# VectorE's order written out for the whole ramp, one pair of maxima moved into the ramp, and weight loads due in slots 5 to 12 issued in slot 13

## The chip, the cores and the metric

The kernel runs on one core of one Trainium2 chip. The metric is the device time of one execution in microseconds (us). The kernel before takes 1043.43 us (median of 3 runs, 1042.8 to 1046.78).

## The reference

Two branches share one layer norm, and both are added to the input:

```python
xn = _layernorm(x, axis=-1)                       # x: 2048 tokens x 640
return x + _A_ref(xn, A_wqkv, A_wo) + _B_ref(xn, B_w_gate, B_w_up, B_w_down)
```

Branch A is attention with 32 heads of 20 columns; each query sees the 256 keys up to and including its own:

```python
scores = jnp.einsum("bhqd,bhkd->bhqk", q, k) * (Dh ** -0.5)
mask = (idx[:, None] - idx[None, :] >= 0) & (idx[:, None] - idx[None, :] < W)   # W = 256
p = _softmax(jnp.where(mask[None, None], scores, -1e9), axis=-1)
```

Branch B is a gated feed-forward part, `h = gelu(g) * u`, of width 1728. All tensors are float32.

## The kernel before

**Stages.** The 2048 tokens are four chunks of 512 (c = 0 to 3). First comes the *ramp* (`first_chunk`, L345, the loop behind it, L460, and twelve steps of filler at the head of `attention()`, L832): layer norm, transposes of the normed tiles, first projections. Then `attention()` (L823) works through 32 *units* u (8 groups of four heads times 4 chunks), each cut into 14 *slots* i; T = 14 u + i counts slots. Dense projections ("filler") are pulled in between so that TensorE (PE) never lacks work. After that come the feed-forward part and the output sums, which the change does not touch.

**Dense products.** An operand is split into a high and a low fp32r part, and `dense_steps` (L104) issues three blocks of five matmuls, weight by input: high by high, low by high, high by low (so `xl` is read in the last block). `proj_qk` (L240) makes one 128-row slice of q (t below 5) or k (t from 5) for a chunk in a PSUM bank `ps_d` (pool `psd`, two banks). `proj_v` (L315) makes `ps_v` for one tile of 128 tokens.

**What follows a projection.** `save_qk` (L248) cuts q or k into three bf16 parts: ScalarE (ACT) writes the first into `pt` (L277), VectorE (DVE) subtracts it into `r` (L273), ACT writes the second (L255), GpSimd (POOL) the third (L259), and SyncE (SP) stores `pt` to DRAM (`qd` or `kd`, L268). `r` has one buffer, so the next L273 waits until POOL has read the last one; `pt` has two, so an L277 waits for the store of the tile before last. `load_stack` (L478) reads q and k back from DRAM into `qs` (three buffers) and `ks` (four) three units ahead, in slots 9 (`ks`) and 12 (`qs`).

**Layer norm in the ramp.** Per tile of 128 tokens `xi`, DVE computes statistics (L149 to L151), per chunk the scale (L156 to L165), per tile the normed values (L169). PE transposes them into `ps_t` (L185), ACT writes the high part `xh` (L193), DVE the low part `xl` (L194). In `first_chunk` (L345) every engine's order is written out by hand; after it a scheduler sets the order of all engines in the ramp, mixing statistics of chunks 2 and 3 with other work of DVE.

**Maxima.** `max_pair` (L493) makes two PSUM banks of masked scores `ps_m` (L512, pool `psm`, four banks, shared with transposes), and DVE reduces each to its row maxima (L522). Eight pairs make a unit. Pairs are pulled ahead of the unit in which they serve: by `pull_max` in the ramp's last part (L832: 12 steps of filler, two pairs in each even step) and in slots 0, 5 and 9, twice in slot 0, and once in T = 3. In a slot, `exp_piece` (L563) then issues scores `ps_e` (L577) for ACT's exponentials (L579).

**Weight loads.** When chunk 0 of a filler set is done, `load_qk` (L232) or `load_gu` (L640) at once issues two loads `wr` of 320 KB for the next set on SP, whatever the slot. `split_later` (L651) has ACT read them (L656) once chunk 1, then chunk 2 of the set is done, some 14 slots later each. SP issues all these DMAs in the order of the program, on one queue.

Of the kernel before, what the change touches and what calls it, by code (L numbers as in the profile page):

```python
# [20 lines left out]
NC = S // C  # L21
# [46 lines left out]
def block_kernel(ctx, tc, x, wqk, wv, wgu, wdo, wdl, out):  # L68
# [99 lines left out]
    def ln_apply(xi, mv, rs):  # L168
        nc.vector.tensor_scalar(xi, xi, mv[:, 0:1], rs, op0=OP.subtract, op1=OP.mult)  # L169

    def ln_scale(xs, lp, mv=None, begun=0):
        n = len(xs)
        mv = mv or lp.tile([128, n, 2], F32, name="mv4", tag="mv4", bufs=2)
        for i in range(begun, n):
            ln_stats(xs[i], mv[:, i, :], lp)
        rs = ln_rstd(*ln_sqrt(mv, n, lp), n, lp)
        for i, xi in enumerate(xs):
            ln_apply(xi, mv[:, i, :], rs[:, i:i + 1])

    def turn(k, xs, where):  # L180
        n = len(xs)
        pool, tag = {"x": (psx, "ex"), "m": (psm, "mx"), "o": (psm, "mx")}[where]
        ps = pool.tile([128, n * 128], F32, name="ps_t", tag=tag)
        for i in range(n):
            nc.tensor.transpose(ps[:, i * 128:(i + 1) * 128], xs[i][:, k * 128:(k + 1) * 128], ident)  # L185
        return ps

    def ln_turn(t0, xs, where="xmxmx"):
        n = len(xs)
        cs = slice(t0 * 128, (t0 + n) * 128)  # L190
        for k in range(KT):
            ps = turn(k, xs, where[k])
            nc.scalar.activation(xh[:, k, cs], ps, AF.Copy)  # L193
            nc.vector.tensor_tensor(out=xl[:, k, cs], in0=ps, in1=xh[:, k, cs].bitcast(F32), op=OP.subtract)  # L194

    acts = {}
    done = set()
# [27 lines left out]
    def behind(fn, *a):  # L225
# [3 lines left out]
        else:  # L229
            fn(*a)  # L230

    def load_qk(t):  # L232
        raw = wrp.tile([128, KT, 128], F32, name="wr", tag="wr")
        nc.sync.dma_start(raw, wqk[t])
        return raw

    def split_qk(raw):
        return split(wp, raw, [128, KT, 128], "wq", nc.gpsimd)
# [106 lines left out]
    def first_chunk(xs, wr0, wr5, prep, v0, lp):  # L345
        halves = slice(0, 256), slice(256, 512)

        def low(k, ps, cs):
            nc.vector.tensor_tensor(out=xl[:, k, cs], in0=ps, in1=xh[:, k, cs].bitcast(F32), op=OP.subtract)

        def high(k, ps, cs):
            nc.scalar.activation(xh[:, k, cs], ps, AF.Copy)

        def part(ps, w, r, cs, first=False, last=False, ks=range(KT)):
            for k in ks:
                nc.tensor.matmul(ps[:, cs], w[:, k, :], r[:, k, cs], start=first and k == 0,  # L356
                                 stop=last and k == KT - 1, skip_group_check=True)

        def high_qk(raw):
            wh = wp.tile([128, KT, 128], F32R, name="wqh", tag="wqh")  # L360
            nc.scalar.activation(wh, raw, AF.Copy)
            return wh

        def low_qk(raw, wh):
            wl = wp.tile([128, KT, 128], F32R, name="wql", tag="wql")
            nc.gpsimd.tensor_tensor(out=wl, in0=raw, in1=wh.bitcast(F32), op=OP.subtract)
            return wh, wl

        def hold(xi):
            nc.gpsimd.tensor_copy(one[:, 0:1], xi[:, 0:1])  # L370

        with tc.manual_schedule(engines=MANUAL | {mybir.EngineType.Pool}):
            mv = [lp.tile([128, 2, 2], F32, name="mv", tag="mv", bufs=2) for _ in range(2)]
            ln_stats(xs[0], mv[0][:, 0, :], lp)
            ln_stats(xs[1], mv[0][:, 1, :], lp)
            rs = ln_rstd(*ln_sqrt(mv[0], 2, lp), 2, lp)
            ln_apply(xs[0], mv[0][:, 0, :], rs[:, 0:1])
            ln_apply(xs[1], mv[0][:, 1, :], rs[:, 1:2])
            wh0 = high_qk(wr0)
            hold(xs[1])  # L380
            w0 = low_qk(wr0, wh0)
# [36 lines left out]
            part(dn[1], w5[1], xh, halves[1])  # L418
            part(dn[1], wh5, xl, halves[1], last=True)
            mv = lp.tile([128, 4, 2], F32, name="mv4", tag="mv4", bufs=2)  # L420
            for j in range(4):
                ln_stats(xs[4 + j], mv[:, j, :], lp)
            rs = ln_rstd(*ln_sqrt(mv, 4, lp), 4, lp)
            for i in range(2):
                for _ in proj_v(v0, i, (psm, "mx")):
                    pass
            for j in range(4):
                ln_apply(xs[4 + j], mv[:, j, :], rs[:, j:j + 1])
            save_qk(0, 0, dn[0])
            mv = lp.tile([128, 4, 2], F32, name="mv4", tag="mv4", bufs=2)  # L430
            for j in range(2):
                ln_stats(xs[8 + j], mv[:, j, :], lp)
        save_qk(5, 0, dn[1])
        return w0, w5, v0, mv

    v0 = []
    with tc.tile_pool(name="lp", bufs=1, side="right") as lp:
# [15 lines left out]
        w0, w5, v0, mv = first_chunk(xs, wr0, wr5, prep, v0, lp)  # L453
        ones = lp.tile([4, 2 * C], BF, name="ones")
        nc.gpsimd.memset(ones, 0.0)
        nc.gpsimd.memset(ones[0:2], 1.0)
        for i in range(NK):
            for j in (0, 2):
                nc.sync.dma_start(ks[i][SR:64, j:j + 2].rearrange("p j t -> p (j t)"), ones)
        for c in range(1, NC):  # L460
            if c > 1:
                ln_scale(xs[4 * c:4 * c + 4], lp, *((mv, 2) if c == 2 else ()))
            ln_turn(4 * c, xs[4 * c:4 * c + 4], "xmxmx" if c == NC - 1 else "xmxmm")
            if 1 < c < NC - 1:
                xs += [ln_load(t, lp) for t in range(4 * c + 4, 4 * c + 8)]
            if c == 1:
                for i in range(NQ):
                    for j in (0, 2):
                        nc.sync.dma_start(qs[i][SR + 2:64, j:j + 2].rearrange("p j t -> p (j t)"), ones[2:4])
            if c == 2:  # L470
                raws1 = [load_qk(1), load_qk(6)]
            if c < NC - 1:
                run(*[proj_v(v0, 4 * c - 4 + i, None if i % 2 else (psm, "mx")) for i in range(0 if c > 1 else 2, 4)])
                run(proj_qk(0, w0, c), proj_qk(5, w5, c))
# [165 lines left out]
    def load_gu(f):  # L640
        raws = []
        for i in range(2 if f < NF - 1 else 1):
            raw = wrp.tile([128, KT, 128], F32, name="wr", tag="wr")
            nc.sync.dma_start(raw, wgu[2 * f + i])
            raws.append(raw)
        return raws

    def split_gu(pools, raws):
# [174 lines left out]
    def attention():  # L823
# [8 lines left out]
        for i in range(12):  # L832
# [3 lines left out]
            if i == 0:  # L836
                pull_max(1, now[0])
                pull_fill(RAMP)
                pull_max(1, now[0])
                debt[0] -= RAMP  # L840
            elif i % 2 == 0:
                pull_max(2, now[0])
            flush()
            pull_fill(2 * RAMP)
# [688 lines left out]
```

## Time and profile before

| | |
|---|---|
| Median of 3 runs | 1043.43 us |
| Profiled execution, its own time | 1043.06 us |
| Span in the trace | 1041.3 us |
| Time around the span | 1.76 us |
| PE busy | 1031.8 us (99%) |
| VectorE busy | 740.3 us (71%) |
| ScalarE busy | 527.9 us (51%) |
| GpSimd busy | 384.5 us (37%) |

A timeline row reads: start, duration, engine, line, operation, out<-in, count, and in brackets the idle time of that engine just before it and what ended it. A wait row reads: engine and line that waited, what it waited for, the total, the number of waits, the longest. A windows row gives the stretch, then each engine's busy time, the granted PE clock, the busy share of the DMA engines and GB/s. A PE row's duration reaches past the start of the next row, since matmuls are pipelined; the step from start to start is what a row takes of the engine.

### The profile page before, as it was taken

Reading aid. Unit: us, or ns where it says so; the run is one execution under the profiler, and the core shown is the slowest. Engines: PE = TensorE matmul, PEld = TensorE weight load, DVE = VectorE, ACT = ScalarE, POOL = GpSimd, SP = SyncE. Lnnn points to the kernel's source line nnn. Section 1 sums busy time; section 2 is a strip of 40 time slices with the busy share of each in tenths; the row PEclk is TensorE's granted clock in tenths of the full one; section 3 lists DMA queues with packets and bytes.
Section 4 is the critical chain, followed back from the end, with each engine's and each line's share of the span. In section 5 each row is a group of like instructions: output and inputs, shape, how many; then the busy total and the mean of one; then the engine's idle time right before and its main releaser. Section 6 shows DMA issues by size and latency. Waiting matters only on the chain.

```text
span 1041.3 us, 25568 instructions
## 1 busy us (share of the span) xinstructions
PE 1031.8 (99%) x9396; PEld 834.4 (80%) x9396; DVE 740.3 (71%) x2018; ACT 527.9 (51%) x1120; POOL 384.5 (37%) x623
## 2 busy tenths in 40 slices
PE   9999999999999999999999999999999999999998
PEld 8887666666777666666678888888888999999998
DVE  7855666677656576777736778776556888888887
ACT  4434766767666666666675322223324544333332
POOL 5122778988765787766461111101110000000000
PEclk9999999999999999999999999999999999999999
DMA  6642356564633455343325576673117874433333
GB/s 224 182 144 70 110 157 182 160 181 142 185 98 99 117 150 163 94 145 109 99 76 190 187 248 212 246 256 110 72 58 268 252 244 138 137 128 111 127 122 105
DMA packets 102150, 158.74 MB, mean 152 GB/s; under 512 B 14172, under 2 KB 55260, under 8 KB 102024
## 3 DMA queue, kind: packets, MB, share of 16 engines
q1 hardware_dynamic: 99640, 150.94, 45.7%
q10 hardware_dynamic: 2384, 6.16, 1.9%
q8 instruction: 74, 1.21, 0.5%
q14 instruction: 52, 0.43, 0.1%
HBM read 101.78 MB, written 54.92 MB: 150 GB/s over the span
## 4 chain that ended last, share of the span: by engine, by line
PE 92%; DVE 5%; DMA 1%; issue 1%; ACT 1%; SPq 0%; DVEq 0%; ACTq 0%
PE ps_g L977 24%; PE ps L1249 23%; PE ps_d L108 19%; PE ps_e L577 8%; PE ps_v L108 6%; PE ps_o L620 5%; PE ps_m L512 5%; DVE junk L522 2%; PE ps_g L108 1%; PE ps_d L356 1%; DVE xi L169 0%; DMA qs<-qd 0%; PE ps_t L185 0%; DVE st L150 0%; DVE xl L194 0%
## 5 line engine op out<-in xcount | busy, mean ns | idle before, releaser
L522 DVE CUSTOM_DVE_ANT_0 junk<-ps_m,mask 128x320 bf16<-128x320 f32 (+2 forms) x512 | 242.5, 474 | 132.1 <-PE ps_m L512 73.6
L579 ACT ACTIVATE P<-ps_e 128x512 f32<-128x512 f32 (+2 forms) x384 | 198.7, 572 | 65.3 <-PE ps_e L577 64.6
L1249 PE MATMUL ps<-wb,at 128*128 128x320 f32 x999 | 155.9, 309 | 0.0
L1249 PEld LDWEIGHTS ps<-wb,at 128*128 128x128 f32 x999 | 148.9, 188 | 0.2
L592 POOL TENSOR_SCALAR_AFFINE_SELECT P<-P 128x256 f32<-128x256 f32 (+1 forms) x192 | 94.7, 495 | 72.4 <-ACT P L579 71.6
L577 PE MATMUL ps_e<-qs,ks 124*128 124x128 bf16 (+2 forms) x704 | 118.3, 278 | 0.1
L108 PE MATMUL ps_d<-xl,wqh 128*128 128x512 f32 x310 | 98.5, 421 | 0.0
L108 PE MATMUL ps_d<-xh,wqh 128*128 128x512 f32 x310 | 98.3, 421 | 0.0
L108 PE MATMUL ps_d<-xh,wql 128*128 128x512 f32 x310 | 97.6, 418 | 0.0
L101 POOL TENSOR_TENSOR wql<-wr,wqh 128x640 fp32r<-128x640 f32 x12 | 19.2, 1607 | 195.4 <-PE ps_g L977 150.8
L1249 PE MATMUL ps<-wt,at 128*128 128x320 f32 x552 | 88.9, 309 | 0.0
L577 PEld LDWEIGHTS <-ks 124*128 124x128 bf16 x704 | 49.5, 98 | 49.0 <-issue 34.4
L1249 PEld LDWEIGHTS ps<-wt,at 128*128 128x128 f32 x552 | 82.9, 188 | 0.1
L595 POOL TENSOR_SCALAR_AFFINE_SELECT P<-P 128x512 f32<-128x512 f32 (+1 forms) x144 | 76.8, 542 | 16.3 <-ACT P L579 16.3
L1203 ACT ACTIVATE at<-ss 128x512 fp32r<-128x512 f32 x59 | 37.3, 632 | 83.3 <-DVE ss L1082 83.3
L620 PE MATMUL ps_o<-P,v 64*32 64x320 f32 (+4 forms) x2816 | 74.2, 347 | 0.0
L259 POOL TENSOR_TENSOR pt<-r,pt 128x512 bf16<-128x512 f32 x40 | 46.7, 1167 | 64.4 <-ACT pt L255 64.0
L620 PEld LDWEIGHTS ps_o<-P,v 64*32 64x32 f32 x2816 | 50.8, 106 | 21.5 <-issue 0.9
L512 PE MATMUL ps_m<-ks,qs 60*64 60x320 bf16 (+3 forms) x1472 | 64.0, 260 | 3.2 <-DMA qs<-qd 1.1
L108 PEld LDWEIGHTS ps_d<-xh,wql 128*128 128x128 f32 x310 | 56.0, 189 | 10.2 <-issue 1.3
L1006 ACT ACTIVATE hr<-hr 128x512 f32<-128x512 f32 x20 | 12.6, 632 | 101.6 <-DVE hr L980 101.6
L108 PEld LDWEIGHTS ps_d<-xh,wqh 128*128 128x128 f32 x310 | 56.0, 189 | 9.8 <-issue 1.6
(197 smaller groups left out, 1981.6 us busy)
## 6 DMA issues: line engine op xcount, KB each, us to landing
hd<-he SPq DMA_DIRECT2D x50, 256.0 KB
hr<-hd SPq DMA_DIRECT2D x48, 256.0 KB
wr<-wgu SPq DMA_DIRECT2D x27, 320.0 KB
qs<-qd SPq DMA_DIRECT2D x64, 120.0 KB
ks<-kd SPq DMA_DIRECT2D x64, 120.0 KB
xi<-x SPq DMA_DIRECT2D x16, 320.0 KB
qs<-qd SPq DMA_DIRECT2D x64, 80.0 KB
ks<-kd SPq DMA_DIRECT2D x64, 80.0 KB
```

What stands on the lines that cost most here:

```text
L108: nc.tensor.matmul(ps, a(k), b(k), start=n == 0, stop=n == 3 * nk - 1)
L259: nc.gpsimd.tensor_tensor(out=pt[:, l, :], in0=r, in1=pt[:, 1, :], op=OP.subtract)
L512: nc.tensor.matmul(ps[64 * h:64 * h + 64, col:col + w], q[rows, j, q0:q0 + 64], ks_, start=True, stop=True, tile_position=(64 * r, 64 * h))
L522: nc.vector.tensor_tensor_reduce(out=junk[:, 0:n], in0=ps[:, 320 - n:320], in1=mask[:, 320 - n:320], scale=1.0, scalar=NEG, op0=OP.add, op ...
L577: nc.tensor.matmul(ps[:, col:col + n], k[0:QROWS, j, kc:kc + 128], q[0:QROWS, j, q0:q0 + n], start=True, stop=True)
L579: nc.scalar.activation(pt[:, j, lo:hi], ps[:, lo:hi], AF.Exp, scale=SCALE)
L592: nc.gpsimd.affine_select(out=a, in_=a, pattern=[[0, n], [1, 128]], compare_op=OP.is_ge, fill=0.0, base=0, channel_multiplier=-1)
L595: nc.gpsimd.affine_select(out=a, in_=a, pattern=[[0, n], [-1, 128]], compare_op=OP.is_ge, fill=0.0, base=-1, channel_multiplier=1)
L620: nc.tensor.matmul(os[r][32 * j:32 * j + 32, qa:qb], v[rows, w0_:w0_ + 32], pt[rows, j, col + qa - q0:col + qb - q0], start=r not in begun ...
L977: nc.tensor.matmul(ps, i, j, start=first and n == 0, stop=n == len(work) - 1, skip_group_check=True)
L1203: nc.scalar.activation(hi[:, 3:7], s, AF.Copy)
L1249: nc.tensor.matmul(ps[bank][:, 0:HD], *work[bank][j], start=bank not in begun, stop=final[p, bank] == n and j == len(work[bank]) - 1, skip ...
```

## The change

Four edits. (1) In the ramp after `first_chunk`, DVE's order is now the program's. The program text is rearranged so that statistics of a chunk's first two tiles (`ln_begin`) come in fixed places, the rest of the layer norm of chunk c + 1 (`ln_scale`) right behind chunk c's `xl`, and the second part of k's first slice (`save_qk(5, 0)`) between the third and fourth `xl` of chunk 1. (2) The fifth transpose of chunk 3 goes to a bank of pool `psd` ("d") and not `psx`. (3) Two pairs of maxima are pulled in the ramp's last step (i = 11), and none in T = 3. (4) A load `wr` that falls due in slots 5 to 12 is issued in slot 13 of the same unit.

```diff
-    def ln_scale(xs, lp, mv=None, begun=0):
+    def ln_begin(xs, lp):
+        mv = lp.tile([128, 4, 2], F32, name="mv4", tag="mv4", bufs=2)
+        for i in range(2):
+            ln_stats(xs[i], mv[:, i, :], lp)
+        return mv
+
+    def ln_scale(xs, lp, mv):
         n = len(xs)
-        mv = mv or lp.tile([128, n, 2], F32, name="mv4", tag="mv4", bufs=2)
-        for i in range(begun, n):
+        for i in range(2, n):
             ln_stats(xs[i], mv[:, i, :], lp)
...
+    def load_later(src):
+        raw = wrp.tile([128, KT, 128], F32, name="wr", tag="wr")
+        i = 0 if now[0] is None or now[0] < 0 else now[0] % NS
+        if i > 4:
+            at(now[0] + NS - 1 - i, lambda: nc.sync.dma_start(raw, src))
+        else:
+            nc.sync.dma_start(raw, src)
+        return raw
...
+            mv = ln_begin(xs[8:], lp)
             save_qk(0, 0, dn[0])
...
-        save_qk(5, 0, dn[1])
-        return w0, w5, v0, mv
+        return w0, w5, v0, mv, dn[1]
...
-        for c in range(1, NC):
-            if c > 1:
-                ln_scale(xs[4 * c:4 * c + 4], lp, *((mv, 2) if c == 2 else ()))
-            ln_turn(4 * c, xs[4 * c:4 * c + 4], "xmxmx" if c == NC - 1 else "xmxmm")
...
+        with tc.manual_schedule(engines={mybir.EngineType.DVE}):
+            for c in range(1, NC):
+                ln_turn(4 * c, xs[4 * c:4 * c + 4], "xmxmd" if c == NC - 1 else "xmxmm",
+                        (lambda: save_qk(5, 0, k_first)) if c == 1 else None)
+                if c == NC - 1:
+                    break
+                ln_scale(xs[4 * c + 4:4 * c + 8], lp, mv)
...
+                run(proj_qk(0, w0, c))
+                if c == 1:
+                    mv = ln_begin(xs[12:], lp)
+                run(proj_qk(5, w5, c))
...
-            elif i % 2 == 0:
+            elif i % 2 == 0 or i == 11:
                 pull_max(2, now[0])
...
-                if i in (0, 5, 9) or T == 3:
+                if i in (0, 5, 9):
                     pull_max(2, T)
```

Three places show how the order of the instructions moves. The first is VectorE in the ramp, at the normalization of chunk 2. `mv_556` (before) and `mv_548` (after) hold chunk 2's statistics, `mv_910` those of chunk 3. Before:

```order
L149 BN_STATS st<-xi 128x6
L163 TENSOR_TENSOR ve<-ve,rs 128x4
L150 BN_STATS st<-xi 128x6
L273 TENSOR_TENSOR r<-ps_d,pt 128x512
L164 SCALAR_TENSOR_TENSOR ve<-ve,rs 128x4
L151 BN_AGGR mv_910<-st 128x2
L149 BN_STATS st<-xi 128x6
L165 SCALAR_TENSOR_TENSOR rs<-ve,rs 128x4
L150 BN_STATS st<-xi 128x6
L169 TENSOR_SCALAR xi<-xi,mv_556,rs 128x640 x3
L273 TENSOR_TENSOR r<-ps_d,pt 128x512
L169 TENSOR_SCALAR xi<-xi,mv_556,rs 128x640
```

And after, where `mv_721` holds chunk 3's statistics:

```order
L151 BN_AGGR mv_548<-st 128x2
L156 TENSOR_TENSOR ve<-mv_548,one 128x4
L162 RECIPROCAL rs<-sq 128x4
L163 TENSOR_TENSOR ve<-ve,rs 128x4
L164 SCALAR_TENSOR_TENSOR ve<-ve,rs 128x4
L165 SCALAR_TENSOR_TENSOR rs<-ve,rs 128x4
L169 TENSOR_SCALAR xi<-xi,mv_548,rs 128x640 x4
L287 TENSOR_TENSOR r<-ps_d,pt 128x512
L149 BN_STATS st<-xi 128x6
L150 BN_STATS st<-xi 128x6
L151 BN_AGGR mv_721<-st 128x2
```

The four normalizations of chunk 2 now stand ahead of both subtractions `r` of chunk 1 and of all statistics of chunk 3. The second place is TensorE behind the ramp's last regular pairs (`ps_m<-ks_180,qs_177`, step i = 10). Before, filler runs up to slot 0 of unit 0, whose pairs begin with `ks_179`:

```order
L512 MATMUL ps_m<-ks_180,qs_177 64x320
L108 MATMUL ps_d<-xl_80,wqh 128x512 x4
L108 MATMUL ps_d<-xh_76,wqh 128x512 x5
L108 MATMUL ps_d<-xh_76,wql 128x512 x5
L108 MATMUL ps_d<-xl_80,wqh 128x512 x5
L108 MATMUL ps_v<-wvh,xh_79 128x320 x5
L108 MATMUL ps_v<-wvh,xl_83 128x320 x5
L108 MATMUL ps_v<-wvl,xh_79 128x320 x5
L108 MATMUL ps_v<-wvh,xh_79 128x320 x5
L512 LDWEIGHTS qs_177
L512 MATMUL ps_m<-ks_179,qs_177 64x256
```

After, the same pairs come eight filler matmuls behind those of i = 10:

```order
L527 MATMUL ps_m<-ks_180,qs_177 64x320
L108 MATMUL ps_d<-xl_80,wqh 128x512 x4
L108 MATMUL ps_d<-xh_76,wqh 128x512 x4
L527 LDWEIGHTS qs_177
L527 MATMUL ps_m<-ks_179,qs_177 64x256
```

All later pairs up to T = 3 move up by one place, and T = 3 has none. The third place is SyncE in unit 4, at the first of the four pairs of loads that move. Before:

```order
L487 DMA ks_182<-kd_91 60x1024
L234 DMA wr<-wqk 128x640 x2
L268 DMA qd_84<-pt 64x3x512 x2
L487 DMA qs_177<-qd_87 40x1024
L487 DMA qs_177<-qd_87 20x1024
L487 DMA qs_177<-qd_87 60x1024
```

After:

```order
L502 DMA qs_177<-qd_87 40x1024
L502 DMA qs_177<-qd_87 20x1024
L502 DMA qs_177<-qd_87 60x1024
L243 DMA wr<-wqk 128x640 x2
L282 DMA kd_88<-pt 64x3x512 x2
L775 DMA td_102<-tx 128x256
```

The two loads are now behind the store `qd_84` and all six `qs_177` loads, and directly ahead of the store `kd_88`. The other three pairs of loads that move (units 8, 12 and 21) also go behind the `qs` loads of their unit.

More of the change, by code (lines that the diff above doesn't have):

```diff
@@ L181, in turn @@
         n = len(xs)
-        pool, tag = {"x": (psx, "ex"), "m": (psm, "mx"), "o": (psm, "mx")}[where]
+        pool, tag = {"x": (psx, "ex"), "m": (psm, "mx"), "o": (psm, "mx"), "d": (psd, "dn")}[where]
         ps = pool.tile([128, n * 128], F32, name="ps_t", tag=tag)
@@ L186, in turn, with ln_turn @@
         return ps
-    def ln_turn(t0, xs, where="xmxmx"):
+    def ln_turn(t0, xs, where, mid=None):
         n = len(xs)
@@ L194, in ln_turn @@
             nc.vector.tensor_tensor(out=xl[:, k, cs], in0=ps, in1=xh[:, k, cs].bitcast(F32), op=OP.subtract)
+            if k == 2 and mid:
+                mid()
     acts = {}
@@ L230, in behind @@
             fn(*a)
+    def load_later(src):
[6 more added lines that the diff above has]
+        return raw
     def load_qk(t):
-        raw = wrp.tile([128, KT, 128], F32, name="wr", tag="wr")
-        nc.sync.dma_start(raw, wqk[t])
-        return raw
+        return load_later(wqk[t])
     def split_qk(raw):
@@ L428, in first_chunk @@
                 ln_apply(xs[4 + j], mv[:, j, :], rs[:, j:j + 1])
+            mv = ln_begin(xs[8:], lp)
             save_qk(0, 0, dn[0])
-            mv = lp.tile([128, 4, 2], F32, name="mv4", tag="mv4", bufs=2)
-            for j in range(2):
-                ln_stats(xs[8 + j], mv[:, j, :], lp)
-        save_qk(5, 0, dn[1])
-        return w0, w5, v0, mv
+        return w0, w5, v0, mv, dn[1]
     v0 = []
@@ L452, in block_kernel @@
         xs += [ln_load(t, lp) for t in range(4, 8)]
-        w0, w5, v0, mv = first_chunk(xs, wr0, wr5, prep, v0, lp)
+        w0, w5, v0, mv, k_first = first_chunk(xs, wr0, wr5, prep, v0, lp)
         ones = lp.tile([4, 2 * C], BF, name="ones")
@@ L459, in block_kernel @@
                 nc.sync.dma_start(ks[i][SR:64, j:j + 2].rearrange("p j t -> p (j t)"), ones)
-        for c in range(1, NC):
-            if c > 1:
-                ln_scale(xs[4 * c:4 * c + 4], lp, *((mv, 2) if c == 2 else ()))
-            ln_turn(4 * c, xs[4 * c:4 * c + 4], "xmxmx" if c == NC - 1 else "xmxmm")
[L464 to L472, printed above, removed]
+        with tc.manual_schedule(engines={mybir.EngineType.DVE}):
[6 more added lines that the diff above has]
+                if c == 1:
+                    xs += [ln_load(t, lp) for t in range(12, 16)]
+                    for i in range(NQ):
+                        for j in (0, 2):
+                            nc.sync.dma_start(qs[i][SR + 2:64, j:j + 2].rearrange("p j t -> p (j t)"), ones[2:4])
+                else:
+                    raws1 = [load_qk(1), load_qk(6)]
                 run(*[proj_v(v0, 4 * c - 4 + i, None if i % 2 else (psm, "mx")) for i in range(0 if c > 1 else 2, 4)])
-                run(proj_qk(0, w0, c), proj_qk(5, w5, c))
+                run(proj_qk(0, w0, c))
+                if c == 1:
+                    mv = ln_begin(xs[12:], lp)
+                run(proj_qk(5, w5, c))
     vtiles = dict(enumerate(v0[2]))
@@ L642, in load_gu @@
         for i in range(2 if f < NF - 1 else 1):
-            raw = wrp.tile([128, KT, 128], F32, name="wr", tag="wr")
-            nc.sync.dma_start(raw, wgu[2 * f + i])
-            raws.append(raw)
+            raws.append(load_later(wgu[2 * f + i]))
         return raws
```

## The prediction

> **What bounds the kernel now.** I read the page's first part, then TensorE's waits, then its timeline around each of them, then the engine or queue that ended each.
>
> ```profile
> PE 1031.8 (99%) x9396; PEld 834.4 (80%) x9396; DVE 740.3 (71%) x2018; ACT 527.9 (51%) x1120; POOL 384.5 (37%) x623
> ```
>
> TensorE (PE) is busy 1031.8 of 1041.3 us, and the change removes none of its matmuls. All that can be won is PE's idle time, 1041.3 - 1031.8 = 9.5 us, and the little that hides in rows stretched by a wait. Its waits, without that for the very first operand:
>
> ```profile
> PE ps_t L185 <- DVE xi L169: 1.2, 3, 0.8
> PE ps_m L512 <- DMA qs<-qd: 1.1, 2, 0.6
> PE ps_m L512 <- DVE mx L522: 0.6, 2, 0.4
> PE ps_t L185 <- DVE xl L194: 0.2, 1, 0.2
> PE ps_m L512 <- DVE xl L194: 0.2, 1, 0.2
> ```
>
> They make 1.2 + 1.1 + 0.6 + 0.2 + 0.2 = 3.3 us; the rest of the idle time has no wait named. The reader sees three that weigh: transposes waiting for normed tiles (edit 1 touches it), maxima waiting for `qs` (edit 4) and for earlier maxima (edit 3); edit 2 touches the fourth row.
>
> **Edit 1, VectorE's order.** PE around the transposes of chunk 1 (24.18) and of chunk 2 (38.56 to 41.25):
>
> ```profile
> 24.18 2.34 PE L185 MATMUL ps_t<-ident,xi 128*128 128x128 f32 x20
> 26.28 0.97 PE L108 MATMUL ps_v<-wvh,xh 128*128 128x320 f32 x5
> ...
> 38.56 2.03 PE L185 MATMUL ps_t<-ident,xi 128*128 128x128 f32 x15 [0.82 <-DVE xi L169]
> 40.35 0.54 PE L108 MATMUL ps_v<-wvh,xh 128*128 128x320 f32 x2
> 40.73 0.77 PE L185 MATMUL ps_t<-ident,xi 128*128 128x128 f32 x5
> 41.25 0.69 PE L108 MATMUL ps_v<-wvh,xh 128*128 128x320 f32 x3
> ```
>
> Unhindered, 20 transposes step 26.28 - 24.18 = 2.10 us. In chunk 2 they step (40.35 - 38.56) + (41.25 - 40.73) = 2.31, after 0.82 of idle time. Excess: 0.82 + 0.21 = 1.03 us. What VectorE (DVE) did before:
>
> ```profile
> 18.98 0.44 DVE L149 BATCH_NORM_STATS2 st<-xi 128x6 f32<-128x320 f32 x1
> ...
> 19.84 0.21 DVE L151 BATCH_NORM_AGGREGATE mv<-st 128x2 f32<-128x12 f32 x1
> ...
> 21.29 2.18 DVE L169 TENSOR_SCALAR xi<-xi,mv,rs 128x640 f32<-128x640 f32 x4
> 26.01 0.69 DVE L273 TENSOR_TENSOR r<-ps_d,pt 128x512 f32<-128x512 f32 x1 [2.54 <-issue]
> ...
> 29.57 2.43 DVE L194 TENSOR_TENSOR xl<-ps_t,xh 128x512 fp32r<-128x512 f32 x4
> ...
> 37.19 2.37 DVE L169 TENSOR_SCALAR xi<-xi,mv,rs 128x640 f32<-128x640 f32 x3
> ```
>
> DVE idles 2.54 us at 23.5. One tile's statistics take 19.84 + 0.21 - 18.98 = 1.07 us, so the two tiles that now come first fit there (2.1 us), and `r` behind them starts where it did, near 26. Chunk 1's two `r` (0.69 each) and five `xl` (0.61 each: 2.43 / 4) take 4.4 us; I add 0.6 because the second `r` must let ACT and POOL finish with the first (one buffer). The `xl` then end near 31 (before: 29.57 + 2.43 = 32.0). Two tiles of statistics 2.1, the scale 1.24 (21.29 - 20.05), four normalizations 2.18: the last is ready near 36.5. PE asks at 38.56 - 0.82 = 37.7. With 1.2 us of slack the **1.03 us** go.
>
> What was pushed back, chunk 1's two `r` of the next projections and chunk 3's first statistics, ends about 36.5 + 2 x 0.69 + 2.1 = 40, and chunk 2's `xl` (five of 0.61) by 43 to 44. PE's reader of those is the last block of the projections that begin here:
>
> ```profile
> 33.05 1.30 PE L108 MATMUL ps_d<-xl,wqh 128*128 128x512 f32 x5
> ...
> 49.84 1.32 PE L108 MATMUL ps_d<-xh,wqh 128*128 128x512 f32 x5
> ```
>
> So they have cover to 50 us; chunk 1's `xl`, ending near 31, to 33.05. The moves cost nothing while that cover stands; past it each us is PE's.
>
> **Edit 2, the bank of the fifth transpose.** It ends one wait and uncovers the next:
>
> ```profile
> 57.62 0.69 DVE L273 TENSOR_TENSOR r<-ps_d,pt 128x512 f32<-128x512 f32 x1 [2.71 <-ACT pt L277]
> 58.23 3.19 DVE L194 TENSOR_TENSOR xl<-ps_t,xh 128x512 fp32r<-128x512 f32 x5
> ...
> 58.97 0.66 PE L185 MATMUL ps_t<-ident,xi 128*128 128x128 f32 x4 [0.20 <-DVE xl L194]
> ...
> 60.88 0.31 PE L512 MATMUL ps_m<-ks,qs 60*64 60x64 bf16 x5 [0.18 <-DVE xl L194]
> ```
>
> At 58.97 the fifth transpose waited for the first `xl` to free its bank. At 60.88 the second pair waited for the fourth `xl` (58.23 + 4 x 0.64 = 60.8). DVE's chain starts with `r`, which waits for ACT behind the end of PE's projection, and that chain is unchanged; PE merely waits longer at the second place. I cost the edit at nothing; bounds 0 and -0.38, the two rows.
>
> **Edit 3, the pairs of T = 3.**
>
> ```profile
> 82.57 0.49 DVE L522 CUSTOM_DVE_ANT_0 junk<-ps_m,mask 128x320 bf16<-128x320 f32 x1
> ...
> 83.22 0.49 DVE L522 CUSTOM_DVE_ANT_0 junk<-ps_m,mask 128x320 bf16<-128x320 f32 x1
> ```
>
> ```profile
> 89.08 0.47 PE L512 MATMUL ps_m<-ks,qs 60*64 60x256 bf16 x16
> 89.48 0.85 PE L108 MATMUL ps_v<-wvh,xl 128*128 128x320 f32 x4
> ...
> 93.50 0.58 PE L512 MATMUL ps_m<-ks,qs 60*64 60x256 bf16 x9
> 94.51 0.33 PE L512 MATMUL ps_m<-ks,qs 60*64 60x128 bf16 x7 [0.43 <-DVE mx L522]
> 94.77 0.39 PE L577 MATMUL ps_e<-qs,ks 124*128 124x256 bf16 x2
> ```
>
> The 16 matmuls of slot 5 step 94.77 - 93.50 = 1.27 us where those of slot 0 step 0.40: one maximum steps 83.22 - 82.57 = 0.65 us, two pairs 2.6, so three pulls in five slots outrun DVE and fill the four banks. Without the pull of T = 3 this is -0.87 us. In step i = 11 the two pairs come eight filler matmuls behind those of i = 10, 2 us by the row at 49.84 (1.32 / 5 each); DVE, which needs 2.6 from the first bank on, may hold the last bank a little longer than PE's own 0.40 allows: 0 to 0.2 lost. Otherwise the pairs cost PE the same there, plus one more change between filler and maxima, 0 to 0.1. I take +0.1 together: **-0.8 us**.
>
> **Edit 4, the loads.** Unit 4, the first of four places, then the `qs` loads of unit 8, where the `wr` loads had gone 5.8 us earlier (213.4) and were through:
>
> ```profile
> 157.91 0.86 SPq L234 DMA_DIRECT2D wr<-wqk  x2
> 158.88 1.32 SPq L268 DMA_DIRECT2D qd<-pt  x2
> 160.30 4.74 SPq L487 DMA_DIRECT2D qs<-qd  x6
> ...
> 219.21 2.14 SPq L487 DMA_DIRECT2D qs<-qd  x6
> ...
> 158.90:161.20 2.30, 2.30 (x85) 1.51 (x86) 1.55 (x7) 0.00 (x0) 2.30 (x4) 1.00 0.98 302
> ...
> 166.32 0.27 PE L512 MATMUL ps_m<-ks,qs 60*64 60x256 bf16 x1 [0.60 <-DMA qs<-qd]
> 167.10 0.47 PE L512 MATMUL ps_m<-ks,qs 60*64 60x256 bf16 x15 [0.51 <-DMA qs<-qd]
> ```
>
> The loads keep the DMA engines 98% busy from 158.9 to 161.2 (640 KB at 302 GB/s are 2.2 us), the six `qs` issues behind them take 4.74 us and not 2.14, and PE then waits 0.60 + 0.51 = **1.11 us** for `qs`. With the loads behind them, `qs` is issued 0.97 us earlier (158.88 - 157.91) and has 2.2 us less traffic ahead: 3 us, more than the wait. The other three places show no wait of PE for `qs`, so nothing there.
>
> The Trainium skill ("DMA: Bandwidth & Descriptors", section "Queues, rings and completion order") says that each DMA engine consumes a ring's descriptors in ring order; the trace agrees, `qs` issues stretching from 2.14 to 4.74 us behind `wr`. By that rule the same 2.2 us move onto the store `kd`, the rival below.
>
> What the loads now delay is ACT, their reader, and the `pt` store behind them:
>
> ```profile
> 227.17 0.59 ACT L277 ACTIVATE pt<-ps_d 128x512 bf16<-128x512 f32 x1
> 227.65 0.73 ACT L656 ACTIVATE wqh<-wr 128x640 fp32r<-128x640 f32 x1
> ```
>
> In unit 8 `wr` will be issued near 219.21 + 2.14 = 221.4, done near 222.3, and take 2.2 us (the rate above) to 4.74 (the stretched issue as a bound): landed by 224.5 to 227, ahead of 227.65. The `kd` store behind it frees the `pt` that ACT writes at 227.17: 2.2 us later than before it can be just late. I take 0; bounds 0 and 2.5 us, in each of units 4 and 8.
>
> **Sum.** -1.03 + 0 - 0.8 - 1.11 = -2.9 us against the profiled 1043.06 us (span 1041.3 and 1.76 around it): **1040.2 us**. The median of the runs, 1043.43, is 0.4 above that execution. The gain is 0.3%, less than the 0.5% (5.2 us) that a measurement of this kernel can tell from no change.
>
> **The rivals.**
> - *The wait for `qs` stays* (the stretched issue has another cause, such as a reader of the buffer): -1.8 us, 1041.2. For it: SP issues `qs` behind other waits as well. Against: the DMA engines are full just then.
> - *Given back at the `pt` store:* the `kd` store, now behind `wr`, lands after ACT wants its `pt` (227.17 in unit 8, the like in unit 4). ACT, its exponentials and PE wait up to 2.5 us in each unit; half of that makes 1040.2 + 2.5 = 1042.7.
> - *Slower: the same store in full.* From 1.5 us of delay in each of the two units the change loses more than its 2.9 us; at 2.5 in each it is 1043.06 - 2.9 + 5.0 = 1045.2. For it: no cover is visible beyond that row of ACT. Against: two units only, and PE holds filler while ACT waits.
> - *A blocked VectorE.* Written out, DVE's order lets a late `r` hold `xl`. If chunk 1's second `r` waits for POOL, its `xl` end later than 31 us, and PE's block at 33.05 needs them: from 2 us of extra wait PE loses each us in full. The nearest row is DVE's 2.71 us for ACT: 0.7 lost there, edit 1's 1.03 not won, 1043.06 - 1.9 + 0.7 = 1041.9. The Trainium skill ("TensorE: Matmul & The Clock Gate", section "What's actually happening") halves PE's clock after an idle window of about 3.4 us; no wait here is longer than 1.2 us and the granted clock is 1.00 in the row at 158.90, so only a longer block would add to it.
> - *Hidden anyway:* each wait returns at the next limit, as in edit 2: 1043.
>
> **Chances.** Forecast (1039.3 to 1040.9) 0.57; `qs` wait stays 0.13; given back 0.10; blocked VectorE 0.05; hidden anyway 0.05; slower 0.05; more than the sum (edit 2's 0.38 and 1.4 of stretched rows like those of edits 1 and 3: 1038.4) 0.05. The range 1038.4 to 1044.0 holds all but the slower case and the noise of a run. Faster by over 0.5% needs 5.2 us where the named waits hold 3.3: the upper part of the last case, 0.04. Slower by over 0.5% needs 8 us of new waits against the gain, the slower case and more of it: 0.04. Within: 0.92.
>
> **What would show it.** Right: no idle time before chunk 2's transposes, their 20 in one row; slot 5 of unit 0 stepping 0.4 us; no wait of PE for `qs`, and PE idle near 7 us. Edit 2 right: the wait at the second pair grows to some 0.4 us. Wrong: ACT's L277 (now L291) waiting for the `kd` store near 170 or 226 us, ACT's read of `wr` waiting, or a gap of PE in 31 to 37 us.

## The result and the profile after

The changed kernel takes 1039.85 us (median of 8 runs, 1039.25 to 1041.25) against 1043.12 us of the kernel before beside it (8 runs): ratio 0.9968, 95% interval 0.9955 to 0.9982. The profiled execution took 1039.31 us, span 1037.6, that is 3.7 us less span than the profiled execution before. The forecast was 1040.2 us and -2.9 us.

The page's first row and TensorE's (PE's) waits after (engine and line that waited, what for, total, times, longest):

```profile
PE 1031.2 (99%) x9396; PEld 834.9 (80%) x9396; DVE 741.0 (71%) x2018; ACT 526.8 (51%) x1120; POOL 383.6 (37%) x623
```

```profile
PE ps_t L190 <- DVE xi L169: 0.2, 1, 0.2
PE ps_m L527 <- DVE xl L199: 0.2, 1, 0.2
```

Without that for the very first operand these are all. PE's idle time fell from 9.5 to 1037.6 - 1031.2 = 6.4 us. The waits for normed tiles (but 0.2 us), for `qs` and for earlier maxima are gone.

**Edit 1.** PE's timeline after, from the last block of chunk 1's projections to chunk 2's first:

```profile
36.29 1.30 PE L108 MATMUL ps_d<-xl,wqh 128*128 128x512 f32 x5
37.43 2.35 PE L190 MATMUL ps_t<-ident,xi 128*128 128x128 f32 x20
39.53 0.98 PE L108 MATMUL ps_v<-wvh,xh 128*128 128x320 f32 x5
...
48.41 1.32 PE L108 MATMUL ps_d<-xh,wqh 128*128 128x512 f32 x5
```

The 20 transposes stand in one row, without idle time, and step 39.53 - 37.43 = 2.10 us. VectorE (DVE) over the same time, from the end of chunk 1's `xl` on:

```profile
28.71 1.28 DVE L199 TENSOR_TENSOR xl<-ps_t,xh 128x512 fp32r<-128x512 f32 x2
...
33.25 2.18 DVE L169 TENSOR_SCALAR xi<-xi,mv,rs 128x640 f32<-128x640 f32 x4
...
38.38 0.69 DVE L287 TENSOR_TENSOR r<-ps_d,pt 128x512 f32<-128x512 f32 x1 [0.32 <-ACT pt L291]
38.98 3.19 DVE L199 TENSOR_TENSOR xl<-ps_t,xh 128x512 fp32r<-128x512 f32 x5
```

Chunk 1's `xl` end at 28.71 + 1.28 = 30.0 us (estimated 31), the last normed tile at 35.4 (36.5), chunk 2's `xl` at 42.2 (43 to 44). PE asks for the normed tiles at 37.43, so they have 2.0 us to spare.

**Edit 2.** Chunk 3's transposes and the first pairs of maxima, after:

```profile
55.24 2.35 PE L190 MATMUL ps_t<-ident,xi 128*128 128x128 f32 x20
...
57.70 1.41 PE L108 MATMUL ps_d<-xh,wqh 128*128 128x512 f32 x4
59.05 0.21 PE L527 MATMUL ps_m<-ks,qs 60*64 60x64 bf16 x1
59.44 0.31 PE L527 MATMUL ps_m<-ks,qs 60*64 60x64 bf16 x5 [0.18 <-DVE xl L199]
```

The wait ahead of the fifth transpose is gone, and the second pair waits 0.18 us as before; what was won turns up in the row at 57.70, whose four matmuls step 59.05 - 57.70 = 1.35 us. Before, the same four stepped 60.48 - 59.38 = 1.10:

```profile
59.38 1.17 PE L108 MATMUL ps_d<-xh,wqh 128*128 128x512 f32 x4
60.48 0.21 PE L512 MATMUL ps_m<-ks,qs 60*64 60x64 bf16 x1
```

**Edit 3.** Slot 5 of unit 0 steps 92.56 - 92.15 = 0.41 us where it stepped 1.27:

```profile
92.15 0.47 PE L527 MATMUL ps_m<-ks,qs 60*64 60x256 bf16 x16
92.56 0.39 PE L592 MATMUL ps_e<-qs,ks 124*128 124x256 bf16 x2
```

**Edit 4.** SP's queue in unit 4 and PE's pair that reads this `qs`:

```profile
156.66 2.94 SPq L502 DMA_DIRECT2D qs<-qd  x6
159.65 1.32 SPq L243 DMA_DIRECT2D wr<-wqk  x2
```

```profile
163.03 0.47 PE L527 MATMUL ps_m<-ks,qs 60*64 60x256 bf16 x16
```

The loads stand behind `qs`, and the pair has no wait. In unit 8, where the `kd` store now stands behind the loads, ACT (its timeline) goes from `pt` to `wr` without idle time:

```profile
223.08 0.59 ACT L291 ACTIVATE pt<-ps_d 128x512 bf16<-128x512 f32 x1
223.56 0.73 ACT L669 ACTIVATE wqh<-wr 128x640 fp32r<-128x640 f32 x1
```

The margin of that store is thin: by the landing times in the trace its last transfer came in at 222.90 us, 0.18 ahead of ACT's `pt` at 223.08.

So far the prediction seems right in nearly every line. One profile of each kernel can't tell, however, whether a wait that is gone was there because of the edited code or in that execution only; the runs below were made for that.

### The profile page after: what moved, and what is told of

It reads as the page before. It is cut to its first block, busy times and chain, and to the rows that moved or that the text cites. A ratio compares the mean times of both kernels' runs of the same rounds, so it can differ in the third digit from the quotient of the medians.

```text
span 1037.6 us, 25574 instructions
## 1 busy us (share of the span) xinstructions
PE 1031.2 (99%) x9396; PEld 834.9 (80%) x9396; DVE 741.0 (71%) x2018; ACT 526.8 (51%) x1120; POOL 383.6 (37%) x623
## 4 chain that ended last, share of the span: by engine, by line
PE 95%; DVE 3%; issue 1%; ACT 0%; DMA 0%; DVEq 0%; ACTq 0%
PE ps_g L990 24%; PE ps L1262 23%; PE ps_d L108 21%; PE ps_e L592 8%; PE ps_v L108 7%; PE ps_o L635 6%; PE ps_m L527 5%; DVE junk L537 2%; PE ps_g L108 1%; PE ps_t L190 1%; PE ps_d L370 1%; DMA xi<-x 0%; DVE xi L169 0%; DVE xl L199 0%; PE ps_n L554 0%
```

## The experiments

Two theories stand against each other. **A:** the gain is the sum of three waits, each removed by its own edit, as predicted. **B:** some of it isn't tied to the edit that stands beside it: a wait of the profile before that belonged to one execution, or a gain that is handed on to the next wait. Medians; the ratio, with its interval, is the recorded one of all runs and not the quotient of two medians, and it is to runs of the kernel before on the same chip (1042.44 us, 33 runs, for the first four kernels, 1042.48, 18 runs, for the others):

| Kernel | Median (runs), us | Ratio to before, 95% | Span of the profile |
|---|---|---|---|
| edit 1 alone | 1040.86 (11) | 0.9991 (0.9980 to 1.0003) | 1038.8 |
| edit 3 alone | 1041.20 (11) | 0.9990 (0.9981 to 0.9999) | 1039.0 |
| edit 4 alone | 1042.21 (11) | 1.0000 (0.9992 to 1.0009) | 1041.2 |
| all but edit 2 | 1040.25 (11) | 0.9981 (0.9972 to 0.9990) | 1039.4 |
| before, a second profile | 1042.07 (1) | | 1040.4 |
| all but edit 4 | 1040.16 (12) | 0.9975 (0.9966 to 0.9984) | 1038.3 |
| all four, again | 1039.40 (7) | 0.9968 (0.9955 to 0.9981) | 1037.6 |
| all four and filler | 1036.96 (6) | 0.9945 (0.9929 to 0.9960) | 1035.1 |

The intervals are about as wide as the effects, so the verdicts rest on steps from row to row in the profiles.

### Edit 1 alone

The changed kernel with edits 2 to 4 taken back:

```diff
-    "xmxmd" if c == NC - 1
+    "xmxmx" if c == NC - 1
-    elif i % 2 == 0 or i == 11:
+    elif i % 2 == 0:
-    if i in (0, 5, 9):
+    if i in (0, 5, 9) or T == 3:
-    if i > 4:              (load_later)
+    if False:
```

> The kernel before with edit 1 alone (VectorE's order and the rearranged layer norm; no "d" bank, no pair moved, loads as before). Theory A, the edits stand apart: PE's idle of 0.82 us on L169 ahead of chunk 2's transposes is gone, the step from the start of the last dense block before them to the next projection falls from 13.39 to about 12.1 us, and nothing behind it changes: span about 1.3 us below that of before, some 1040.0 (time 1041.8). The stall of 0.87 us in slot 5 of unit 0 and the two waits for qs (0.60 and 0.51 us) are still there. Rival B, a gain is handed on: PE comes 1.3 us earlier to the same late qs or to VectorE's maxima, waits that much longer there, and the span falls by less than 0.5 us.

PE's timeline at the two rows between which edit 1 acts:

```profile
36.72 1.30 PE L108 MATMUL ps_d<-xl,wqh 128*128 128x512 f32 x5
...
48.85 1.32 PE L108 MATMUL ps_d<-xh,wqh 128*128 128x512 f32 x5
```

The step to the next projection is 48.85 - 36.72 = 12.13 us (before: 13.39, from 36.45 to 49.84), and the stall in slot 5 is still there: edit 1 gives its 1.26 us by itself, and A is right on it. But neither theory had the span of 1038.8, 2.5 us below the first profile of before. What came on top is above all the wait for `qs`, which is gone with the loads still ahead of it on SP's queue:

```profile
156.41 0.86 SPq L245 DMA_DIRECT2D wr<-wqk  x2
...
158.80 3.24 SPq L502 DMA_DIRECT2D qs<-qd  x6
```

PE's pair that reads this `qs` starts at 164.31 with no wait. In the trace's DMA records the last transfer of `qs` starts at 163.86; in the first profile of before the first one starts at 162.38 and the last at 166.92, and PE had wanted them near 165.7.

### Edit 3 alone

```diff
-    elif i % 2 == 0:
+    elif i % 2 == 0 or i == 11:
-    if i in (0, 5, 9) or T == 3:
+    if i in (0, 5, 9):
```

> The kernel before with edit 3 alone (two pairs in the ramp's last step, none in T = 3). Theory A: the stall of 0.87 us in slot 5 of unit 0 goes, the pair moved costs at most 0.1 us where it now stands, span 0.7 to 0.8 us below before, some 1040.5 (time 1042.3); the wait of 0.82 us on L169 and the waits for qs stay as they were. Rival B: VectorE's maxima are late elsewhere, a stall of 0.4 us or more stands at the moved pair or in slot 9, and the span falls by under 0.4 us.

PE's pair in slot 5 of unit 0:

```profile
93.67 0.47 PE L512 MATMUL ps_m<-ks,qs 60*64 60x256 bf16 x16
94.07 0.39 PE L577 MATMUL ps_e<-qs,ks 124*128 124x256 bf16 x2
```

From the row of chunk 3's projection behind the first pairs (61.17; before 61.11) to the end of this slot it is 94.07 - 61.17 = 32.90 us, before 94.77 - 61.11 = 33.66: 0.76 us, as A said. The wait of 0.81 us for normed tiles stays. Here too the wait for `qs` is gone, with the loads in their old place.

### Edit 4 alone

The kernel before with `load_later` for both kinds of load, as in the change.

> The kernel before with edit 4 alone (loads of slots 5 to 12 in slot 13). Theory A, as predicted: the waits for qs (1.11 us) and the stretched matmuls beside them go, 1.1 to 1.5 us, and some 0.2 us is lost near 265 us as in the changed kernel: span about 1.2 us below before, some 1040.1 (time 1041.9). The stalls at 151 and 154 us (0.2 and 0.45 us), which stand ahead of these loads, stay. Rival B: those stalls come from the loads too and go with them, span 1.8 us below. Rival C: without the other edits PE arrives later, the qs wait is only partly due to the loads, and under 0.6 us is gained.

PE's timeline ahead of chunk 2's transposes and at the pair that reads `qs`:

```profile
39.03 2.03 PE L185 MATMUL ps_t<-ident,xi 128*128 128x128 f32 x15 [1.40 <-DVE xi L169]
...
166.13 0.47 PE L519 MATMUL ps_m<-ks,qs 60*64 60x256 bf16 x16
```

No wait for `qs`, but the median is within 0.25 us of that of before (ratio 1.0000, with an interval of 0.9 us to either side), and 0.6 us more are lost ahead of chunk 2's transposes, in code that edit 4 doesn't touch. VectorE's timeline shows how: its old order has statistics of chunk 3 ahead of the end of chunk 2's scale (L165), and here they waited for an input tile:

```profile
36.63 0.49 DVE L149 BATCH_NORM_STATS2 st<-xi 128x6 f32<-128x320 f32 x1 [0.30 <-DMA xi<-x]
37.04 1.02 DVE L165 SCALAR_TENSOR_TENSOR rs<-ve,rs 128x4 f32<-128x4 f32 x1
```

(L165 took 0.14 us in the first profile; why 1.02 here isn't settled.) From the first unit to the last this profile keeps the same distance to the second profile of before, below (0.5 us behind it): where the wait doesn't occur, the loads' place is worth nothing, which comes nearest to rival C (under 0.6 us gained).

### The kernel before, a second profile

> The kernel before, unchanged, a second profile. Theory A, the waits for qs (1.11 us) of the first profile are the rule for loads issued ahead of qs: PE waits for qs between 0.9 and 1.3 us again near 166 us, span about 1041. Theory B, the qs load was late in that one execution only, since its transfers ran from 162.38 to 166.92 us (4.5 us) and not the 3.0 to 3.3 us of the two kernels that kept the loads ahead of qs: no wait for qs over 0.3 us here, span 1039.6 to 1040.6.

PE's timeline at edit 1's place, at a stall of unit 4 and at the pair that reads `qs`:

```profile
38.45 2.03 PE L185 MATMUL ps_t<-ident,xi 128*128 128x128 f32 x15 [0.81 <-DVE xi L169]
...
155.01 0.33 PE L512 MATMUL ps_m<-ks,qs 60*64 60x320 bf16 x3 [0.35 <-DVE mx L522]
...
165.63 0.47 PE L512 MATMUL ps_m<-ks,qs 60*64 60x256 bf16 x16
```

The wait for normed tiles and the stall of unit 4 are there again, the wait for `qs` isn't: B. Unit by unit the two profiles agree within 0.1 us until the pair at 165.6 and lie 1.4 to 1.5 us apart from there to the last unit. The 1.11 us that the prediction gave to edit 4 (and 0.35 of stretched rows beside them) belonged to one execution. Of six profiles with the loads ahead of `qs` and nothing else added to the queue, PE waited for it in two: the first one, and all but edit 4, below.

The DMA records show what was late in the first profile: the last 3 of the 256 packets of the two weight loads start only at 163.37 us or later, when the other 253 had ended by 162.51, while in the second profile all had ended by 161.42. A 16 KB packet of kind "instruction" ran from 162.50 to 163.38, just ahead of these three. That it held them up is likely; the records don't say which DMA engine a packet was on.

### All four edits again, and all but edit 2

```diff
-    "xmxmd" if c == NC - 1
+    "xmxmx" if c == NC - 1      (all but edit 2)
```

> The changed kernel, unchanged, beside the ones that leave a part of it out. If the profile of it was typical, its median stays between 1039.3 and 1040.3 and its span between 1037.2 and 1038.2. Edit 2 worth nothing (A): the kernel without it (1040.25, lowest 1040.11) differs by less than 0.6 us, and the gaps between their two profiles stand at VectorE's pauses and not at the bank. Edit 2 worth its 0.3 us or more (B): this one is faster by 0.6 us or more in the lowest and in the median.

> The changed kernel without edit 2 (chunk 3's fifth transpose in psx again). Theory A, edit 2 is worth nothing: span within 0.15 us of the changed kernel's 1037.6, the stretch from chunk 3's first projection block to the next one 11.26 us in both, and time within its interval of 1039.9. Rival B, with the new order of VectorE the bank matters: the wait for the second pair or for the bank grows by 0.3 us or more, span about 1038.0.

All four again: span 1037.6, median 1039.40, the profile was typical. Without edit 2, PE's timeline has, at chunk 2's second row of projections and behind chunk 3's transposes:

```profile
48.78 1.32 PE L108 MATMUL ps_d<-xh,wqh 128*128 128x512 f32 x5
...
60.04 0.50 PE L108 MATMUL ps_d<-xh,wqh 128*128 128x512 f32 x1
```

The stretch is 60.04 - 48.78 = 11.26 us, with edit 2 59.67 - 48.41 = 11.26: at its place the edit is worth 0.00. Yet this kernel is 0.4 to 0.85 us slower by the medians and 1.8 by the span, of which 0.36 stood before 24 us, ahead of all edits; by the times alone that is B's sign (0.6 us or more), and only the rows speak against it. VectorE's instructions are the same, in the same order; only the waits at two maxima of the ramp differ. One thing that moved is a pause of VectorE, which the kernel with edit 2 doesn't have here, and PE's stall behind it:

```profile
116.16 0.49 DVE L537 CUSTOM_DVE_ANT_0 junk<-ps_m,mask 128x320 bf16<-128x320 f32 x1 [0.50 <-DVE mx L537]
```

```profile
117.36 0.33 PE L527 MATMUL ps_m<-ks,qs 60*64 60x320 bf16 x3 [0.35 <-DVE mx L537]
```

Another pause stands at 497.53, ahead of another loss of 0.36. A third loss, 0.5 us at 226 us, is of another kind. ACT's timeline, then PE's:

```profile
224.30 0.60 ACT L291 ACTIVATE pt<-ps_d 128x512 bf16<-128x512 f32 x1 [0.40 <-PE ps_m L527]
```

```profile
226.06 0.86 PE L592 MATMUL ps_e<-qs,ks 124*128 124x128 bf16 x4 [0.22 <-ACT P L594]
```

This is the `pt` of unit 8 that the `kd` store behind the weight loads has to free. The profile names `ps_m`, which this row doesn't read; by the landing times in the trace the store's last transfer came in at 224.20, 0.10 ahead of ACT's start, where in the changed kernel it came in 0.18 ahead of an ACT that didn't wait. So in this execution PE paid 0.5 us for the place of the loads: the prediction's rival "given back at the `pt` store", at a fifth of the 2.5 us it allowed. Of six profiles with edit 4 it is the only one. How much of the difference of the medians comes from the pauses and how much from this store isn't shown.

### All but edit 4

```diff
-    if i > 4:              (load_later)
+    if False:
```

> The changed kernel without edit 4 (loads at once, as before). Theory B, the loads cost margin and seldom time: qs lands 0.2 to 0.6 us before PE wants it, no wait for qs, time within 0.5 us of the changed kernel's (about 1040.0). Theory A, the loads in front of qs cost their 1.1 us each time: PE waits 0.6 us or more for qs, time 1040.8 or more.

PE's timeline at the pair that reads `qs`:

```profile
163.18 0.29 PE L527 MATMUL ps_m<-ks,qs 60*64 60x256 bf16 x1
163.81 0.47 PE L527 MATMUL ps_m<-ks,qs 60*64 60x256 bf16 x15 [0.34 <-DMA qs<-qd]
```

Between A and B: PE waits, but 0.34 us, and loses 0.63 with the step beside it (164.21 - 163.18 = 1.03 where an undisturbed pair steps 0.40). The median is 0.76 us above that of all four beside it, with intervals that overlap, and its fastest run (1039.26) equals the fastest of all four (1039.26): the loss isn't there in every execution. So on top of edits 1 and 3, which bring PE forward, edit 4 is worth 0.63 us in this execution; edits 1 and 3 one by one kept the loads in front and met no wait.

### Pressure on the queue

Both kernels load unit 7's `ks` a second time, ahead of its `qs`; the second one has edit 4 too:

```diff
-    load_stack(u + 3, (int(i == KSLOT),))
+    load_stack(u + 3, (1, 0) if (u, i) == (4, 12) else (int(i == KSLOT),))
```

> The kernel before with a second, needless load of unit 7's ks in slot 12 of unit 4, ahead of its qs on the same queue and behind the two weight loads (six more transfers of some 2.2 us). Ahead of it, with the loads in front of qs, qs landed 0.45 us before PE asked for it in two kernels, 1.3 us after in one and 0.3 us after in another. Theory B (the loads take margin from qs): the margin is used up and PE waits 1.3 to 2.3 us for ks or qs near 166 us. To be read against the next run.

> The kernel before with edit 4 and the same needless load. Theory B: the two weight loads now stand behind qs, whose margin was 1.6 us in the kernel with edit 4 alone, so PE waits 0.2 to 1.1 us, that is 0.7 to 1.3 us less than the run beside it. If the place of the loads on the queue doesn't matter (the traffic alone does), both wait the same within 0.2 us.

PE's timeline with the loads ahead:

```profile
167.41 0.27 PE L512 MATMUL ps_m<-ks,qs 60*64 60x256 bf16 x1 [1.42 <-DMA qs<-qd]
168.88 0.50 PE L512 MATMUL ps_m<-ks,qs 60*64 60x256 bf16 x15 [1.20 <-DMA qs<-qd]
...
170.00 2.06 PE L108 MATMUL ps_d<-xh,wql 128*128 128x512 f32 x4
```

and with the loads behind:

```profile
166.72 0.47 PE L519 MATMUL ps_m<-ks,qs 60*64 60x256 bf16 x15 [0.72 <-DMA qs<-qd]
```

The times are 1046.47 and 1042.76 us (one run each; before beside them 1042.53). The named waits are 2.62 and 0.72 us, 1.9 apart where 0.7 to 1.3 was expected. Since the transfers' own duration varies, their start is the better witness: in the DMA records the first transfer of the needless load comes at 162.64 us, right behind the loads' last one at 162.15, and at 160.57 with the loads behind. The place of the loads costs 2.1 us of margin here (0.2 of it because PE itself is that much later in the first kernel), traffic alone is refuted, and edit 4's mechanism is the predicted one. It is one execution of each kernel. The spans differ by more, 1044.8 against 1041.0, since a second price came on top. The windows of the first kernel (per engine busy time, then the granted PE clock):

```profile
170.00:171.00 1.00, 1.00 (x4) 0.81 (x3) 0.86 (x4) 1.00 (x3) 0.00 (x0) 0.50 0.49 170
171.00:172.00 1.00, 1.00 (x5) 0.48 (x4) 0.54 (x4) 0.56 (x2) 0.35 (x1) 0.50 0.32 94
```

Behind nearly 2.9 us with one matmul in them (166.0 to 168.88) the clock was 0.50 for these two us and 0.60 and 0.69 in the two beside them; the four filler matmuls at 170.00 took 2.06 us, where four took 1.17 at 167.49 in the second kernel.

### VectorE moved on by 60 instructions

```diff
             pull_fill(2 * RAMP)
+            for _ in range(5):
+                nc.vector.memset(dum, 0.0)
```

> The kernel before with 60 memsets of one column on VectorE in the ramp's last part, five in each of its twelve steps, where VectorE is idle for half of the time. In three profiles with the old order of VectorE's work a pause of 0.5 us without a releaser stands between two maxima near 153 us, behind the 446th recorded VectorE instruction, and PE then loses 0.2 and 0.15 to 0.45 us in the pairs of slots 5 and 9 of unit 4. If the pause goes by the count of instructions (P), it now stands behind the same number of instructions, so some 60 instructions of work earlier (near 136 us) and not near 153, and PE's two stalls at 151 to 155 us go: the step from the pair of slot 5 to that of slot 9 of unit 4 falls by 0.2 us. If it goes by that place in the work (W), it stays near 153 us.

A pause of VectorE in the first profile of before, then the one behind the same number of recorded instructions here:

```profile
222.16 0.49 DVE L522 CUSTOM_DVE_ANT_0 junk<-ps_m,mask 128x320 bf16<-128x320 f32 x1 [0.50 <-DVE mx L522]
```

```profile
206.67 0.49 DVE L522 CUSTOM_DVE_ANT_0 junk<-ps_m,mask 128x320 bf16<-128x320 f32 x1 [0.49 <-PE ps_e L577]
```

PE's pair in slot 9 of unit 4:

```profile
154.37 0.78 PE L512 MATMUL ps_m<-ks,qs 60*64 60x320 bf16 x8
155.09 0.61 PE L577 MATMUL ps_e<-qs,ks 124*128 124x128 bf16 x4
```

P in the main: no pause is left near 153 us, which refutes W, and the pause behind number 702 went with the count, from 222.16 us (220.67 in the second profile of before, which lacks the wait for `qs`) to 206.67, some 14 us earlier. But none appeared near 136 us, where the expectation put the one from 153: L532 takes 0.62 us at 136.07, and it took 0.63 at 135.94 in the kernel before, so that isn't the pause, and the maximum behind number 446, now at 138.34, has no idle time before it. PE's pair above steps 155.09 - 154.37 = 0.72 us, in the first profile of before 155.30 - 154.43 = 0.87; the one in slot 5 steps 0.41 and stepped 0.59. But PE loses 0.5, 0.4 and 0.35 us in units 5, 10 and 13, where before it didn't; span 1041.0, 1042.69 us (one run). The shift trades one stall for others.

### Filler ahead of the second pair

What PE still lost most regularly, in both kernels, is this pair behind the short unit of each group (chunk 0), stretched though no wait is named for it, here in the changed kernel:

```profile
101.37 0.92 PE L527 MATMUL ps_m<-ks,qs 60*64 60x320 bf16 x8
102.22 0.96 PE L108 MATMUL ps_d<-xh,wql 128*128 128x512 f32 x3
```

```diff
                     flush()
+                    if (u - 1) % NC == 0:
+                        pull_fill(2)
+                        debt[0] -= 2
                     pull_max(2, T)
```

> The changed kernel with two to three filler matmuls pulled ahead of the second pair of maxima in slot 0 behind each short unit (chunk 0), eight places; the sum of the filler is the same. If those 0.43 us stalls are VectorE's maxima, which get 0.5 to 0.75 us more, each place gains up to 0.43 us: span 2.0 to 3.4 us below the changed kernel's 1037.6, time about 1037.2. If VectorE stays behind and the stall moves on to the next pair in slot 5: within 0.5 us of 1040. Slower by 0.5 us or more if the exponentials of slot 1, which now start 0.6 us later, hold PE for their banks.

PE's timeline at the same pair:

```profile
102.25 0.47 PE L527 MATMUL ps_m<-ks,qs 60*64 60x320 bf16 x8
102.64 0.49 PE L108 MATMUL ps_d<-xh,wql 128*128 128x512 f32 x1
```

The pair steps 102.64 - 102.25 = 0.39 us where it stepped 0.85. Over eight places the span falls by 2.5 us. At 1036.96 us this is the fastest version, 0.9945 (0.9929 to 0.9960) of before; change and filler together gain nearly twice what the change gains alone.

## Why the prediction held, and where it only seemed to

The time came out at -3.3 us by the medians of the first comparison and -3.1 us by those of the second; forecast -2.9. That the sum is so close is in part luck: two of its terms hold, the largest doesn't, and what replaced it wasn't in the sum.

- **Edit 1, -1.03 forecast, -1.27 measured** (13.39 to 12.12 us), and -1.26 alone. The mechanism is the one told. The working counted the wait's idle time and the stretched transposes; left out were the steps from PE's last block to its wait and the extra change between transposes and `ps_v`.
- **Edit 2, 0 forecast, 0.00 measured** at its place (11.26 us with it and without). The stated sign, a wait of 0.4 us at the second pair, was wrong: the lost time stands in a stretched row of filler between two pairs. What the edit does elsewhere, through the places of VectorE's pauses, was not foreseen.
- **Edit 3, -0.8 forecast, -0.77 measured**, -0.76 alone.
- **Edit 4, -1.11 forecast: this term is the step that failed.** It was read as a standing cost of the loads from one execution. A second profile of the same code has no such wait, and the edit alone moves nothing that could be measured. With the other edits it was worth 0.63 us in one execution. The mechanism, two loads ahead of `qs` on one queue, is shown by the pressure pair; its size is a margin, and how often it is overdrawn is known from six profiles only. The edit also takes margin from the `kd` store, which cost 0.5 us in one of six profiles that have it.
- What filled the gap: 0.24 us more from edit 1; 0.35 us of stalls in unit 4 (most of it at 154 us, in the first profile half of it at 151) that stand in the five profiles with VectorE's old instruction count there and in none where the count shifts; and, in the profiles, 0.5 us behind the last unit. The prediction's sum named the maxima's 0.6 us of waits for edit 3 alone, though 0.16 of them was this stall.

So between the second profile of before and the second of after, 1040.4 to 1037.6, the 2.8 us are 2.06 by the end of unit 0 (1.27 + 0.77 and small steps), 0.37 in unit 4, 0.1 lost in later units, and 0.5 gained behind the last unit, where no code differs, with nothing for edit 4, since neither of these two profiles has the wait.

Of the rivals, "the `qs` wait stays" gave 1041.2 and is refuted as to its mechanism; "given back at the `pt` store" gave 1042.7 and didn't happen in either profile of the changed kernel, but its mechanism is real (0.5 us in all but edit 2); VectorE wasn't blocked (0.32 us for ACT at 38.38, with cover). The rule cited from the Trainium skill ("TensorE: Matmul & The Clock Gate", section "What's actually happening") that an idle window of about 3.4 us halves PE's clock played no part in the change, whose granted clock is 1.00 before and after. The pressure run shows the halved clock, 0.50, behind 2.9 us that weren't wholly idle, with one matmul of 0.27 us in them. The rule of ring order ("DMA: Bandwidth & Descriptors", section "Queues, rings and completion order") agrees with the same pair: what stands ahead on the queue delays `qs`.

## What to carry to other kernels

A wait for a DMA in one profile is a draw from a margin: take a second profile before it is priced as a standing cost, and ask how early the transfer lands when it isn't late. Small edits are judged by steps between the same two rows in both traces, not by spans, since here a pause that comes with VectorE's instruction count could cost PE 0.35 us. A load that is moved out of one transfer's way is put in another's: ask for the margin of both. Where one stall recurs at the same place of every period, as behind the short units, a little independent work ahead of it (here 2.4 us in eight places) is worth more than the removal of any one single wait (here at most 1.27).

## What the runs showed of the hardware that was not expected

- VectorE pauses between two maxima without a wait for another engine, at fixed counts. It sits idle for 0.49 to 0.51 us where 0.15 is usual, so the step from one maximum to the next is about 0.35 us longer. Counted from 0 among all records of VectorE in the trace, waits for semaphores included, all 25 such pauses that eleven profiles show stand behind number 62 plus a multiple of 128 (190, 446, 702 and 1214 in before), and a second profile of the same kernel pauses behind the same numbers. Not every such number has one. One of them in the first profile of before:

```profile
79.38 0.49 DVE L522 CUSTOM_DVE_ANT_0 junk<-ps_m,mask 128x320 bf16<-128x320 f32 x1 [0.51 <-DVE mx L522]
```

  Shortly behind the pause near 153 us, the DMA view of 153.5 to 154.2 us has one packet of kind "instruction" on a queue of its own. That suggests the fetch of VectorE's next instructions; it isn't shown. The Trainium skill ("Runtime: NRT & Kernel Launch", section "Instruction fetch mechanics") says that crossing a block of instructions is mostly hidden. If these pauses are such crossings, one that isn't hidden costs VectorE 0.35 us here, and the runs don't settle what decides it.
- The same `qs` load, with the same code ahead of it, took 4.5 us from its first transfer to its last in one execution and 3.0 in another.
